# One branch fewer in a fused RWKV-5 attention and balanced-routing kernel: the test on w joins the check after the first search

## The chip, the cores and the metric

The kernel runs on one core of a Trainium2 chip. A core has five instruction streams: TensorE (PE, with weight loads shown apart as PEld), VectorE (DVE), ScalarE (ACT), GpSimd (POOL) and SyncE (SP), which here issues most of the DMAs. The metric is the device time of one execution in microseconds (us); lower is better. Each stream has its own sequencer, so a branch that all five take is five branches, each taken when that engine gets to it.

## The reference

There are two blocks. The first is RWKV-5 attention over r, k, v of shape (4 batches, 8 heads, 768 steps, 48): a state of 48 by 48 per head decays by w and takes in k and v at every step. The second routes the 3072 tokens to 8 experts, 384 tokens each, greedily by logit, and runs a two-layer ReLU network per expert.

```python
for t in range(S):
    cur = np.einsum('bhd,bhe->bhde', u[None] * kt, vt)
    y[:, :, t] = np.einsum('bhd,bhde->bhe', rt, state + cur)
    state = w[None, :, :, None] * state + np.einsum('bhd,bhe->bhde', kt, vt)
...
order = np.argsort(-flat)
for idx in order:
    tok, e = (int(idx) // E, int(idx) % E)
    if assigned[tok] >= 0 or counts[e] >= cap:
        continue
    assigned[tok] = e
    counts[e] += 1
...
h = np.maximum(x[mask] @ w1[e], 0.0)
out[mask] = h @ w2[e]
```

The inputs have w between 0.85 and 0.95.

## The kernel before

**Two attentions.** The attention works in 24 units, one for each of 6 chunks of 128 steps and 4 batches. `attention_mild` (lines 481 to 685) computes a chunk with powers of w taken from the middle of the chunk, which holds for w between 0.7 and 1.2; `attention_any` (lines 28 to 283) holds for every w and is much longer. `Mild.__init__` (line 293) prepares the tables, counts how many w lie within the bounds, writes the answer into a word called `flag` (line 399), does the first steps of units 0 and 1, and loads the flag into a register of every engine (line 421). Line 1261 then branches on it. These inputs take the first arm, so every engine falls into it, and at its end each engine executes an unconditional branch over the code of the other arm. In the trace both kinds stand as `COMPARE_BRANCH` of line 1261.

**Per unit** TensorE turns r and k (`rows_turned`, `keys_turned`), multiplies pairs (`pairs`, line 526), and forms outputs that stay transposed in `turned[n]` (line 571). VectorE scales k by w (`scale`, line 439), masks the products (line 528) and sums the diagonal (`own`, line 453); GpSimd multiplies r, k and u; ScalarE writes diagonals (line 458) and copies. The order on the engines is written out by hand under `manual_schedule`.

**The first search.** The logits of all tokens lie in `LG`. `Assignment.search` looks for the first expert that fills: `likely` (line 950) runs three rounds of `count` (line 881), each a compare on VectorE, three small products on TensorE, sums on VectorE, one more product, and more sums. Then `tokens` (line 1150) turns the result into a list of token numbers, `tok`. A word, also called flag (line 1032), says whether the quick search was right.

**Rows of x in the search's gaps.** The result of the attention has to lie in DRAM by rows (`x_rows`) before tokens can be gathered from it. `rows` (line 608) takes one unit, turns it with four transposes into one of four PSUM banks, copies it on ScalarE (line 619) and stores it from SP (line 621). Its calls are put into gaps of the search: one unit ahead of the last logits, three after them, then two or three at each `between` inside `count`, and what is left after line 1016. After the last product of `tokens` (line 1177), `between(0)` puts four products on TensorE whose results nobody reads (line 681); five more of this kind follow at line 1438, past the join of the two arms.

**After the search** SP loads the number of the expert and issues the first half of its first weights (line 1229, 768 KB). `settle` (line 921) has GpSimd gather the tokens' rows in three indirect DMAs (line 1238), loads the search's flag on every engine (line 926), and branches (line 928): when the flag is 0, a slow exact search (`surely`) and new gathers are made; these inputs skip that. `leave` (line 937) takes the filled expert out. Then the experts follow: `opening` for the first (transposes of gathered rows at line 1317, their copy by ScalarE at line 1318, products at line 1328), with the search for the next expert between its products.

**Skipping an arm.** A skipped arm leaves no gap in the counting of semaphores: the engine that skips it executes a short block that waits for what it had issued before and adds to each semaphore what the arm would have added. Instructions after the join that follow on memory used in the arm wait for those added counts.

## Time and profile before

| | |
|---|---|
| median of 4 runs | 408.96 us (408.77 to 409.15) |
| the profiled execution | 409.54 us, of which the span of its instructions is 407.8 us |
| granted TensorE clock, mean | 0.997 |
| PE busy | 391.2 us, 96% of the span |
| DVE, ACT, POOL busy | 261.7, 147.1, 118.4 us |
| DMA | 54.43 MB, mean 133 GB/s |

All times below are microseconds from the start of the span. A row of the timeline gives the start of a group of equal instructions, how long it lasted, the engine, the source line, the operation and its tiles; in brackets stands how long the engine had been idle and what ended that. An engine name with a q behind it (SPq, PEldq) is the engine's sequencer: branches, semaphore waits and DMA issues. Matmuls are in float32, so one product of the program stands as two rows of weight loads and two of matmuls.

### The profile page before, as it was taken

The page shows a single profiled execution, that of the slowest core. Times are in us where ns is not written, and L with a number is a line of the kernel's source. Part 1 is how long each engine was busy: PE and PEld are TensorE (multiplying, and loading weights), DVE is VectorE, ACT ScalarE, POOL GpSimd, SP SyncE. Part 2 cuts the span into 40 slices and gives each one's busy share as a digit, 9 for nine tenths or more (in the row PEclk, how much of TensorE's full clock was granted, in tenths as well). Part 3 has the DMA queues.
Part 4 walks back from the last instruction along what each step waited for, and adds up shares of the span by engine and source line. Part 5 has one row for each costly group of instructions (what it writes and reads, how often), then busy time and mean ns, then how long its engine had stood idle before and what let it go on. Part 6 is the DMA issues. An engine that isn't in the chain of part 4 may idle for free. (4 is left out here: it accounts for less than half of the span.)

```text
span 407.8 us, 8503 instructions
## 1 busy us (share of the span) xinstructions
PE 391.2 (96%) x3174; PEld 289.3 (71%) x3174; DVE 261.7 (64%) x767; ACT 147.1 (36%) x378; POOL 118.4 (29%) x154
## 2 busy tenths in 40 slices
PE   7999999999987899999999999999999999999993
PEld 4788888888876585865775785685595586587583
DVE  6997889877567278588478568657856836321021
ACT  3897877878656021212112112112121121211200
POOL 6855775657000302220320320310202122201001
PEclk9999999999999999999999999999999999999998
DMA  8979996810039465614711810830651497201001
GB/s 166 202 146 201 188 197 137 162 34 3 3 130 335 144 233 176 214 39 150 239 39 59 295 73 3 267 129 32 200 188 41 159 341 236 58 21 39 0 21 39
DMA packets 93996, 54.43 MB, mean 133 GB/s; under 512 B 76784, under 2 KB 88176, under 8 KB 93936
## 3 DMA queue, kind: packets, MB, share of 16 engines
q1 hardware_dynamic: 89280, 41.70, 37.1%
q0 software_dynamic: 3072, 9.44, 7.0%
q10 hardware_dynamic: 1584, 2.56, 1.8%
q8 instruction: 29, 0.48, 0.5%
q14 instruction: 31, 0.25, 0.2%
HBM read 44.25 MB, written 9.44 MB: 132 GB/s over the span
## 5 line engine op out<-in xcount | busy, mean ns | idle before, releaser
L1328 PE MATMUL h_ps<-xT,w 128*128 128x384 f32 (+1 forms) x372 | 121.8, 475 | 0.0
L1328 PEld LDWEIGHTS h_ps<-xT,w 128*128 128x128 f32 x372 | 64.6, 190 | 35.9 <-issue 4.0
L1335 ACT ACTIVATE hid<-h_ps 128x384 f32<-128x384 f32 x56 | 27.5, 490 | 114.5 <-PE h_ps L1328 101.0
L1238 POOL DMA_INDIRECT xg<-x_rows,tok x24 | 24.9, 1039 | 144.4 <-issue 121.2
L458 ACT ACTIVATE AT<-ident,dd 128x128 f32<-128x128 f32 x188 | 58.1, 392 | 0.0
L1378 POOL DMA_INDIRECT out_dram<-o_sb,tok x24 | 26.6, 1108 | 104.3 <-DVE o_sb L1428 64.6
L1386 PE MATMUL o_ps<-w,hid 128*128 128x384 f32 x128 | 44.4, 493 | 0.9
L528 DVE COPY_PREDICATED AT<-mask,g_ps 128x512 f32<-128x512 uint8 x48 | 32.6, 732 | 7.5 <-PE g_ps L526 6.7
L1386 PEld LDWEIGHTS o_ps<-w,hid 128*128 128x128 f32 x128 | 23.5, 190 | 18.4 <-issue 4.4
L1407 PE MATMUL o_ps<-T,S 128*128 128x192 f32 x192 | 32.6, 327 | 0.0
L1407 PEld LDWEIGHTS o_ps<-T,S 128*128 128x128 f32 x192 | 31.4, 190 | 0.2 <-DVE S L1399 0.2
L526 PE MATMUL g_ps<-rT,kT 48*128 48x128 f32 x384 | 27.9, 285 | 0.1
L450 POOL TENSOR_TENSOR rk<-rk,u_bc 128x384 f32<-128x384 f32 x24 | 27.3, 1139 | 1.9
L449 POOL TENSOR_TENSOR rk<-rt,kt 128x384 f32<-128x384 f32 x24 | 25.5, 1064 | 5.7 <-DMA rt<-in_r_dram 5.7
L526 PEld LDWEIGHTS g_ps<-rT,kT 48*128 48x128 f32 x384 | 23.3, 187 | 4.1 <-issue 2.9
L571 PE MATMUL y_ps<-AT,vt 128*64 128x128 f32 x368 | 24.6, 276 | 0.0
L1407 PE MATMUL o_ps<-w,hid 128*128 128x192 f32 x128 | 24.6, 326 | 0.0
L1318 ACT COPY xT<-xT_ps 128x384 f32<-128x384 f32 x24 | 10.8, 481 | 34.4 <-PE xT_ps L1317 34.4
L1407 PEld LDWEIGHTS o_ps<-w,hid 128*128 128x128 f32 x128 | 20.9, 190 | 2.1
L470 DVE TENSOR_TENSOR rT<-rT_ps,wr 128x512 f32<-128x512 f32 x24 | 16.5, 687 | 7.6 <-PE rT_ps L465 7.4
L571 PEld LDWEIGHTS y_ps<-AT,vt 128*64 128x64 f32 x368 | 19.7, 137 | 0.9 <-issue 0.3
L1412 DVE TENSOR_TENSOR both<-o_ps,one 128x192 f32<-128x192 f32 x8 | 2.9, 357 | 26.8 <-ACT one L1419 26.8
(237 smaller groups left out, 587.3 us busy)
## 6 DMA issues: line engine op xcount, KB each, us to landing
w<-in_moe_w_dram SPq DMA_DIRECT2D x14, 1536.0 KB, 7.4
kt<-in_k_dram SPq DMA_DIRECT2D x24, 192.0 KB, 3.5
rt<-in_r_dram SPq DMA_DIRECT2D x24, 192.0 KB, 3.7
vt<-in_v_dram SPq DMA_DIRECT2D x24, 192.0 KB, 3.6
x_rows<-AT SPq DMA_DIRECT2D x8, 192.0 KB, 2.8
w<-in_moe_w_dram ACTq DMA_DIRECT2D x1, 1536.0 KB
x_rows<-rt SPq DMA_DIRECT2D x6, 192.0 KB, 3.6
x_rows<-ks SPq DMA_DIRECT2D x5, 192.0 KB, 2.7
```

What stands on the lines that cost most here:

```text
L449: nc.gpsimd.tensor_mul(rk, rt[:, :, 0:D], kt)
L450: nc.gpsimd.tensor_mul(rk, rk, self.u_bc.rearrange("p (h d) -> p h d", h=H))
L458: self.tc.nc.scalar.activation(AT[:, h % 2, h // 2, :], self.ident, AF.Copy, scale=dd[:, h:h + 1])
L526: nc.tensor.matmul(g_pss[q][:, a, :], kT[heads[q], a, :], rT[heads[q], a, :], start=True, stop=True)
L528: nc.vector.copy_predicated(out=AT[:, q], mask=mask.unsqueeze(1).to_broadcast([128, HP, T]), data=g_pss[q])
L571: nc.tensor.matmul(y[j][halves[i], g, :], vt[:, 2 * a + j, :], AT[:, j, a, :], start=(c == 0 and g == 0), stop=(g == 1), skip_group_check= ...
L1238: nc.gpsimd.indirect_dma_start(out=xg[:, c, :], out_offset=None, in_=x_dram, in_offset=bass.IndirectOffsetOnAxis(ap=tok[:, c:c + 1], axis=0))
L1328: product = nc.tensor.matmul(h_ps[:, cols], w1[:, f, ts(j, 128)], xT[:, f, cols], start=(f == 0), stop=(f == KD - 1))
L1335: nc.scalar.activation(hid[:, j, :], h_ps, AF.Relu)
L1378: nc.gpsimd.indirect_dma_start(out=out_rows[n * NC + c], out_offset=bass.IndirectOffsetOnAxis(ap=tok[:, c:c + 1], axis=0), in_=o_sb, in_of ...
L1386: nc.tensor.matmul(o_ps, hid[:, j, ts(c, 128)], w2[:, j, :], start=(j == 0), stop=(j == KF - 1))
L1407: nc.tensor.matmul(part, a[:, j, :], b[:, j, :], start=(j == 0), stop=(j == HF - 1))
```

## The change

1. The branch of line 1261 goes. `Mild` keeps its flag; after the first search a product on VectorE multiplies the search's flag by it, and `settle` of the first search, which had its branch anyway, now also covers a w out of bounds: its body calls `attention_any` first (`anew`) and then the exact search and the gathers. So a chip on which w is within bounds runs one long straight stream from the start to that branch. The branch comes before the pools of the experts are opened, and the gathers stand before it in the same block as the search.
2. `attention_any` no longer borrows memory from `Mild`, nor runs the search itself.
3. `rows` works by half units: 2 transposes a step, the copy and the store after the second half. It is called with 2 and 7 halves around the last logits (1 and 3 units before), with 4 and 7 halves in the gaps of `count` (2 and 3 units before), and with all the rest at the end.
4. The unread products become 9 ahead of the branch (4 before) and 1 after it (5 before).
5. `mild.scale(2)` is tied behind `mild.own(1)`, which is the order that the branch had made, and the zeros of `remainder`, a memset, are computed from `taken`, which keeps them from being moved ahead.

With the branch on w gone, what the skipped body would have done is larger: on SP the short block behind the branch waits for and adds to all eight DMA semaphores that SP uses, that of the half of the weights among them (one semaphore before); on GpSimd, VectorE, ScalarE and TensorE it adds their own counts. In the built program the first copy of gathered rows on ScalarE (line 1318 of the kernel before) waits for these added counts of SP's eight semaphores, of VectorE and of GpSimd; before, it waited for none that an engine adds after this branch, other than TensorE's.

```diff
-            self.holds = nc.values_load(flag[0:1, 0:1])
...
-    todo = iter(range(N))
+    todo = iter([(n, half) for n in range(N) for half in range(2)])
...
-            n = next(todo, None)
+            n, half = next(todo, (None, 0))
...
-            for a in range(HP):
+            for a in (2 * half, 2 * half + 1):
                 nc.tensor.transpose(xr_ps[:, a, :], turned[n][:, a, :], ident)
+            if half == 0:
+                continue
...
             mild.step_products(2)
-            mild.scale(2)
+            with tc.issue_after(mild.summed):
+                mild.scale(2)
...
-            rows(1)
+            rows(2)
             logits(C - 1)
             by_token(C - 1)
-            rows(3)
+            rows(7)
...
         def between(most):
-            rows(most or N)
+            rows({2: 4, 3: 7}.get(most, 2 * N))
             if not most:
-                for _ in range(4):
+                for _ in range(9):
                     nc.tensor.matmul(g_pss[0][:, 0:3, :], ident, ident.unsqueeze(1).to_broadcast([128, 3, 128]),
...
         with self.tc.If(found < 1):
+            if anew:
+                anew()
             with ExitStack() as part:
...
-        nc.vector.memset(sel[:, 1, :], 0.0)
+        nc.vector.tensor_single_scalar(out=sel[:, 1, :], in_=self.taken, scalar=0.0, op=ALU.mult)
...
         walk.search(ahead)
+        nc.vector.tensor_mul(ahead["flag"][0:1, :], ahead["flag"][0:1, :], mild.flag)
         ask_half(ahead["fmax"])
...
+    arguments = tc, r, k, v, w, u, moe_w_gate
     with ExitStack() as part:
-        mild = Mild(part, tc, r, k, v, w, u, moe_w_gate, ident)
-        arguments = (tc, r, k, v, w, u, moe_w_gate, x_dram, LG, ident, walk, first)
-        with tc.If(mild.holds > 0) as branch:
-            with ExitStack() as arm:
-                attention_mild(arm, tc, mild, *arguments[1:])
-        with branch.Else():
-            with ExitStack() as arm:
-                attention_any(arm, mild.vts + mild.rts + mild.kss, mild.ATs[0:2], *arguments)
+        mild = Mild(part, *arguments, ident)
+        with ExitStack() as arm:
+            attention_mild(arm, mild, *arguments, x_dram, LG, ident, walk, first)
+
+    def anew():
+        with ExitStack() as arm:
+            attention_any(arm, *arguments, x_dram, LG, ident, walk)
 
     walk.open(ctx)
+    walk.settle(ahead, ask_half, fetch(xg), asked=True, anew=anew)
...
     awake = ps_t.tile([128, KD, 128], F32, name="xT_ps")
-    for _ in range(5):
-        nc.tensor.matmul(awake, ident, ident.unsqueeze(1).to_broadcast([128, KD, 128]), start=True, stop=True)
-    walk.settle(ahead, ask_half, fetch(xg), asked=True)
+    nc.tensor.matmul(awake, ident, ident.unsqueeze(1).to_broadcast([128, KD, 128]), start=True, stop=True)
```

## The prediction

> **What bounds the kernel now.** I read the page first (busy shares, the chain of waits), then the stages by windows, then the timeline of the stage that the change touches, then the branch instructions by line.

> ```profile
> PE 391.2 (96%) x3174; PEld 289.3 (71%) x3174; DVE 261.7 (64%) x767; ACT 147.1 (36%) x378; POOL 118.4 (29%) x154
> ...
> 114.00:131.30 17.30, 14.13 (x149) 12.12 (x147) 13.63 (x63) 11.12 (x25) 0.00 (x0) 1.00 0.70 251
> 131.30:140.40 9.10, 7.45 (x24) 3.81 (x25) 1.92 (x11) 0.48 (x1) 3.06 (x3) 1.00 0.67 206
> 140.40:158.30 17.90, 17.34 (x120) 13.73 (x120) 12.75 (x52) 4.39 (x9) 0.00 (x0) 1.00 0.47 159
> 158.30:400.00 241.70, 239.97 (x1087) 168.48 (x1088) 141.19 (x447) 43.70 (x94) 46.53 (x43) 1.00 0.37 125
> ```

> Each window's row gives its length, then busy time of PE, PEld, DVE, ACT and POOL. From 140.40 on PE works 257.3 of 259.6 us, so whatever moves the first expert's products moves the end as far. The stretch to read is 131.30 to 140.40: of its 7.45 us of PE work, all but the transposes at 139.16 are unread products.

> ```profile
> 131.26 0.18 PE L1177 MATMUL list_ps<-part,alike 128*128 128x12 f16 x1 [0.57 <-DVE part L1175]
> 131.30 2.83 PE L681 MATMUL g_ps<-ident 128*128 128x384 f32 x8
> 131.92 0.41 SPq L1229 DMA_DIRECT2D w<-in_moe_w_dram  x1
> 134.57 1.17 POOL L1238 DMA_INDIRECT xg<-x_rows,tok  x1 [31.86 <-issue]
> 135.43 3.46 PE L1438 MATMUL xT_ps<-ident 128*128 128x384 f32 x10 [1.31 <-issue]
> 139.16 0.31 PEld L1317 LDWEIGHTS xT_ps<-ident,xg 128*128 128x128 f32 x3 [0.88 <-DMA xg<-x_rows,tok]
> 139.87 0.48 ACT L1318 COPY xT<-xT_ps 128x384 f32<-128x384 f32 x1 [9.53 <-PE xT_ps L1317]
> 140.40 1.42 PEld L1328 LDWEIGHTS h_ps<-xT,w 128*128 128x128 f32 x12 [0.66 <-ACT xT L1318]
> ```

> List of tokens, four unread products, 1.31 us of nothing, five more, then transposes, copy, and the expert's first product at 140.40. The branches, by line:

> ```profile
> L1261 ACTq COMPARE_BRANCH  x1: 38/38/38, 129.9 to 129.9; - x1
> L1261 PEldq COMPARE_BRANCH  x1: 3946/3946/3946, 131.3 to 131.3; - x1
> L1261 DVEq COMPARE_BRANCH  x1: 57/57/57, 131.7 to 131.7; - x1
> L1261 SPq COMPARE_BRANCH  x1: 43/43/43, 132.4 to 132.4; - x1
> ...
> L926 ACTq TENSOR_LOAD <-flag x1: 291/291/291, 132.7 to 132.7; - x1
> L926 SPq TENSOR_LOAD <-flag x1: 281/281/281, 138.5 to 138.5; - x1
> ...
> L928 POOLq COMPARE_BRANCH  x1: 58/58/58, 135.6 to 135.6; - x1
> L928 POOLq EVENT_SEMAPHORE  x1: 43/43/43, 135.8 to 135.8; - x1
> L928 PEldq COMPARE_BRANCH  x1: 242/242/242, 135.9 to 135.9; - x1
> ```

> The reader sees what a jump over an arm costs each sequencer: ACT 129.9 to its next instruction at 132.7, 2.8 us; PE 3.9; DVE from 131.7 to its first wait of line 1122 at 134.7, 2.9; SP, behind its own 768 KB of weights, 132.4 to 138.5, 6.1. GpSimd's short jump of line 928 costs 0.1.

> **The change, part by part.** All times against the profiled execution.

> *The branch at 12 us and its register loads: 0.* DVE goes without a gap through that moment (rows from 11.73, 12.33, 13.15, 13.61 to the masking at 14.43), and PE next waits for that masking (idle 0.17 at 15.84, ended by it). Without that cover it would be worth the 0.27 us that PE idles at 12.79; bounds 0 and a gain of 0.27. SP's load and branch (21.07 to 21.7) go too, so loads start 0.8 us sooner; GpSimd waited for loads at most 3.23 us (25.86), but PE keeps a period of 3.5 and then 4.1 us per unit, so 0. The tie of the third scaling keeps DVE's order: 0.

> *Rows by halves: no PE time, the last store 0.5 sooner.* Before each count PE waits 0.52 to 0.58 us for DVE; one half (2 transposes, 0.22 us) more in it costs nothing. After line 1016 three units are left, not five. ACT's last copy ends near 129.5 in place of 130.34, but SP's issues (0.49 apart, 18 after 120.97) bound the stores, and only its waits for ACT near 125 and 126.5 (0.5 and 0.3) go, so the last issue ends near 130.6 in place of 131.10. The gather waits for these stores: from 134.57 to about 134.0. Bounds 0 and 0.8.

> *The product of the flags: +0.1 on DVE*, queued ahead of `row` in the token list. Nearest rows: the small operations around it start 0.09 to 0.12 apart and last 0.15 to 0.18, so 0.09 to 0.18. The list's product moves from 131.30 to 131.40.

> *Nine unread products, then the branch.* Five take 3.46, four 2.83, so each more 0.63 to 0.65; nine take 6.0, to 137.4. PE's register load (0.31) and jump (3.95) run beside them if the queue takes the products in: 131.4 to about 135.9, 1.5 us of cover. The trace shows seven products of the program queued when PE loads the flag at 158.4. Were only five taken, the jump would start after four have run, at 133.9, and end at 138.2: bounds 0 and 0.8. I take 0, as seven is the nearer. From the end of the products to the next matmul 0.27 (138.89 to 139.16): 137.7. One product: 0.65, to 138.3.

> [...]

> *The transposes:* the first gather's 4.2 us to landing, from 134.0, gives 138.2, so it is in time. Transposes at 138.35, and from their start to the copy 0.71 (139.16 to 139.87): 139.1.

> *The added wait on that copy.* ScalarE now waits until SP and GpSimd have added the skipped counts; behind it in ACT's queue stand the second copy, the issue of the weights' second half and the activations, and PE waits for the copy. SP: weights issued at 131.4, load and branch to 132.3, jump 6.1 (same queue, same 768 KB in front) to 138.4. Then ten waits that add; SP's two of line 928 are 0.1 apart, so 0.6 to 1.0, and I take 0.8: 139.2. One more wait on ACT: the copy at 139.3. With a jump like those of the other engines (2.8 to 3.9) SP would be bound by the landing of the weights (6.2 after issue, 137.6), and PE's 139.1 would decide. GpSimd: load and branch stood 1.08 behind the start of the first gather, so 135.1; its jump over the longer body 2.8 to 2.9 (ACT, DVE): 138.0. Bounds for GpSimd 0.1 (its own row) and 6.1 (SP's).

> [...]

> *DVE* reaches `leave` near 135.8 and not 138.85, worth 0: its first count stands behind nine of the expert's products in PE's order, and the row of the first sum shows it waiting 1.63 us for PE already. *The zeros of `remainder`*: 0.15 on DVE in the last expert's list, beside products; 0 to 0.1.

> *Sum.* The first expert's product follows the copy by 0.53: 139.8 in place of 140.40, 0.6 us sooner; a span of 407.2 and an execution of 408.9 by the profile's own 409.54. That execution stands 0.6 above the median 408.96, so on the median's scale 408.4. Its own range: 408.0 (no replay on the path, 0.2 more; the flags' product free, 0.1; early 0.1) to 408.8.

> **Rivals.** A measurement of this kernel tells about 0.2%, 0.8 us, from no change.

> *Faster by more than that (0.25).* SP's jump is not held up, the flags' product hides, the stores land 0.8 sooner and part of the 0.27 at 12.79 is kept: 0.6 + 0.2 + 0.1 + 0.1, about 408.0, at most 407.7. For it: SP's 6.1 is a single row. Against: each is a bound, not a middle.

> *No gain (0.13).* PE's jump too falls behind the weights, since SP now issues them before PE and DVE branch and not after: 131.8 + 6.1 = 138.0 for PE, product, transposes, copy at 139.6 to 139.8; 408.7 to 408.9. This is also where the queue of five leads.

> *Slower (0.12): the copy waits for GpSimd.* If GpSimd's jump takes SP's 6.1, it adds its count at 141.2, the copy starts at 141.3 against 139.87 and the end comes 1.4 later: 410.4. It decides from a jump of 4.1 on, and slows the kernel from 4.7 on. For it: DMA is 0.67 busy in this stage, and the gathers start together with that jump. Against: the weights' data, by what the jump follows them, have left by then.

> **How the numbers follow.** The middle case has 0.50. Faster by over 0.2% (below 408.14): the first rival and a little of the middle, 0.27. Within: 0.62. Slower (above 409.78): most of the last rival, 0.11. The range is 407.7 to 409.7: below it nothing that I can price, above it the slower half of GpSimd's case.

> **What would show it.** Right: no branch rows near 12 us; nine unread products in one run from 131.4, the next within 0.4 us of their end; the weights issued near 131.4; ACT's copy near 139.3, its long wait ended by SP's added counts; the first expert's product near 139.8, and the rest unchanged. Wrong: an idle PE ahead of the product of line 1437, or a copy that follows GpSimd's branch. The prediction fails if the long straight stream costs PE elsewhere: the periods of 3.5 and 4.1 us per unit, or the 2.3 us that PE idles after 140.40, would then change.

## The result, and the profile after

The changed kernel takes 410.07 us (median of 52 executions, 408.79 to 411.39), the kernel before 409.01 beside it; the ratio is 1.0021 (95% interval 1.0014 to 1.0029). So it is slower by about 0.9 us, where 0.6 faster was forecast. The profiled execution took 410.21 us, its span is 408.5.

The page of the changed kernel, the clock that TensorE was granted, in tenths of full speed and 40 slices of the span:

```profile
PEclk9999999999999899999999999999999999999998
```

One slice has an 8. The same windows as before the change say where (length; busy time of PE, PEld, DVE, ACT, POOL; granted clock; DMA share; GB/s):

```profile
114.00:131.30 17.30, 14.13 (x149) 12.18 (x147) 13.58 (x64) 11.11 (x25) 0.00 (x0) 1.00 0.75 271
131.30:140.40 9.10, 8.80 (x25) 4.83 (x26) 2.95 (x13) 0.00 (x0) 3.06 (x3) 0.81 0.54 170
140.40:158.30 17.90, 17.85 (x118) 13.69 (x117) 11.28 (x48) 4.87 (x10) 0.00 (x0) 1.00 0.42 144
158.30:400.00 241.70, 239.95 (x1092) 168.48 (x1091) 142.04 (x449) 43.69 (x94) 46.16 (x43) 1.00 0.37 126
```

In the stretch that the change touches the clock is 0.81 in place of 1.00, and PE is busy for 8.80 us in place of 7.45. The timeline of that stretch, PE and the copy:

```profile
130.35 0.31 PE L1165 MATMUL some_ps<-vals,row 128*128 128x48 f16 x6 [1.44 <-DVE vals L875]
131.23 0.18 PE L1175 MATMUL list_ps<-part,alike 128*128 128x12 f16 x1 [0.57 <-DVE part L1173]
131.27 7.75 PE L677 MATMUL g_ps<-ident 128*128 128x384 f32 x18
139.31 0.88 PE L1437 MATMUL xT_ps<-ident 128*128 128x384 f32 x2 [0.30 <-PEq L924]
140.03 0.49 PE L1317 MATMUL xT_ps<-ident,xg 128*128 128x128 f32 x3
140.68 0.48 ACT L1318 COPY xT<-xT_ps 128x384 f32<-128x384 f32 x1 [11.25 <-PE xT_ps L1317]
141.21 1.60 PE L1328 MATMUL h_ps<-xT,w 128*128 128x128 f32 x12
```

The nine unread products take 7.75 us, not 6.0. Ahead of the products that make the list (the first row above) PE now idles 1.44 us, where it idled 0.56. In the kernel before, transposes of `rows` stood closer in front of them:

```profile
129.22 0.60 PE L617 MATMUL kv_ps<-ident,xT 128*128 128x128 f32 x4
130.38 0.31 PE L1167 MATMUL some_ps<-vals,row 128*128 128x48 f16 x6 [0.56 <-DVE vals L879]
```

The first expert's product stands at 141.21: 9.98 us behind the list's product (131.23), against 9.14 before (131.26 to 140.40). The branch has this form (line 924; min, median and max over the seven experts, and the first and last start):

```profile
L924 PEldq COMPARE_BRANCH  x7: 202/218/5974, 131.9 to 324.2; - x7
L924 DVEq COMPARE_BRANCH  x7: 56/63/72, 132.3 to 326.3; - x7
...
L924 POOLq COMPARE_BRANCH  x7: 45/45/58, 134.8 to 326.3; - x7
L924 DVEq EVENT_SEMAPHORE  x7: 21/21/21, 137.2 to 326.8; - x7
L924 POOLq INC_SWDGE_SEM  x7: 259/536/904, 138.2 to 326.5; - x7
```

PE's jump, the time that its sequencer needs to go on behind the skipped body, takes 5.97 us (3.95 before); it is over at 137.9, here still beside the slow products. VectorE's lasts from 132.3 to 137.2. GpSimd adds its counts only at 138.2.

The whole span falls into four parts: up to the list's product; from there to the first expert's; from there to the end of PE's last product (the start of its last row in the timeline and its length, 399.63 + 1.46 before, 399.84 + 1.46 after); and what follows. In us, with the kernels of the experiments that come below:

| kernel | list to first expert | to PE's last product | after it | ratio to before |
|---|---|---|---|---|
| before | 9.14 | 260.69 | 6.74 | |
| changed | 9.98 | 260.09 | 7.19 | 1.0021 (1.0014 to 1.0029) |
| whole_rows | 9.32 | 260.61 | 7.19 | 1.0037 (1.0022 to 1.0052) |
| fill_gap | 9.26 | 260.21 | 7.19 | 1.0013 (0.9993 to 1.0032) |
| before_halves | 9.68 | 261.85 | 6.74 | 1.0044 (1.0021 to 1.0067) |
| before_nine | 9.05 | 260.44 | 6.74 | 1.0007 (0.9988 to 1.0026) |
| pad_end | 9.02 | 260.44 | 6.74 | 0.9978 (0.9938 to 1.0017) |
| short_body | 8.29 | 259.61 | 6.71 | one execution, 407.9 us |
| short_body_timed | 8.29 | 259.92 | 6.71 | 0.9963 (0.9943 to 0.9983) |
| act_asks | 10.73 | 260.22 | 7.19 | 1.0072 (1.0034 to 1.0110) |
| no_branch | 8.14 | 259.58 | 6.71 | 0.9952 (0.9938 to 0.9966) |
| before_parts | 8.63 | 261.29 | 6.74 | 0.9995 (0.9974 to 1.0016) |
| late_ask | 10.30 | 260.50 | 6.74 | 1.0047 (1.0025 to 1.0069) |
| parts_late_ask | 8.87 | 261.22 | 6.74 | 0.9993 (0.9971 to 1.0015) |

Between the two profiled executions the changed kernel loses 0.84 in the stage, wins 0.60 in the long part behind it, and loses 0.45 after PE's last product. The first part is the same to 0.03 us.

### The profile page after: what moved, and what is told of

Its sections match the earlier page's. It is cut to its first block, busy times and chain, and to the rows that moved or that the text cites. A ratio compares the mean times of both kernels' runs of the same rounds, so it can differ in the third digit from the quotient of the medians.

```text
span 408.5 us, 8495 instructions
## 1 busy us (share of the span) xinstructions
PE 393.5 (96%) x3176; PEld 290.8 (71%) x3176; DVE 262.9 (64%) x768; ACT 147.1 (36%) x378; POOL 117.4 (29%) x154
## 5 line engine op out<-in xcount | busy, mean ns | idle before, releaser
L1328 PE MATMUL h_ps<-xT,w 128*128 128x384 f32 (+1 forms) x372 | 121.8, 475 | 0.0
L1328 PEld LDWEIGHTS h_ps<-xT,w 128*128 128x128 f32 x372 | 64.6, 190 | 35.9 <-issue 4.0
L1318 ACT COPY xT<-xT_ps 128x384 f32<-128x384 f32 x24 | 10.8, 480 | 36.1 <-PE xT_ps L1317 36.1
```

The source lines that it names most:

```text
L1328: product = nc.tensor.matmul(h_ps[:, cols], w1[:, f, ts(j, 128)], xT[:, f, cols], start=(f == 0), stop=(f == KD - 1))
```

## The experiments

### The clock: an idle gap, or nine products in a run?

Two theories for the clock of 0.81. A: the gap of 1.44 us ahead of the list makes it fall. B: nine such products in a run do. Two kernels take the gap away and keep the nine; two others put the halves alone, and the nine alone, into the kernel before.

```diff
 whole_rows (on the changed kernel)
-            rows(7)
+            rows(6)
-            rows({2: 4, 3: 7}.get(most, 2 * N))
+            rows({2: 4, 3: 6}.get(most, 2 * N))
 fill_gap (on the changed kernel)
-            if not most:
+            if most not in (2, 3):
-                for _ in range(9):
+                for _ in range(9 if not most else 2):
```

> The changed kernel with the rows by whole units again, spread as before the change, so that five units and not three stand after the search's last product and TensorE idles some 0.6 us and not 1.44 us ahead of the list's first product; the nine unread products stay. Theory A (the idle gap of 1.44 us makes the clock gate halve TensorE's clock for 3.4 us, in which the nine products stand: 7.75 us in place of 6.0): granted clock 1.00 from 131.3 to 140.4, the nine products end near 137.3, the first expert's product follows TensorE's branch (137.9) and stands at 140.0 and not 141.2; median 408.6 to 409.0, about 1.2 below the changed kernel. Theory B (nine such products in one run are what makes the clock fall): the clock falls here too, median as the changed kernel, 410.1.

> The changed kernel with two more unread products behind the last unit's transposes, in the idle gap of 1.44 us ahead of the list's first product. Theory A (idle gap): clock 1.00 from 131.3 to 140.4, the first expert's product near 140.0, median 408.6 to 409.0. Theory B (so many unread products close together): the clock falls as in the changed kernel or more, 410.1 or above.

The timeline of PE, whole_rows:

```profile
130.53 0.31 PE L1165 MATMUL some_ps<-vals,row 128*128 128x48 f16 x6 [0.57 <-DVE vals L875]
...
131.46 6.05 PE L677 MATMUL g_ps<-ident 128*128 128x384 f32 x18
138.34 0.88 PE L1437 MATMUL xT_ps<-ident 128*128 128x384 f32 x2 [0.84 <-PEq L924]
```

and of fill_gap:

```profile
129.36 1.46 PE L677 MATMUL g_ps<-ident 128*128 128x384 f32 x4
130.96 0.31 PE L1165 MATMUL some_ps<-vals,row 128*128 128x48 f16 x6
...
131.88 6.05 PE L677 MATMUL g_ps<-ident 128*128 128x384 f32 x18
138.58 0.88 PE L1437 MATMUL xT_ps<-ident 128*128 128x384 f32 x2 [0.65 <-PEq L924]
139.89 0.52 PE L1317 MATMUL xT_ps<-ident,xg 128*128 128x128 f32 x3 [0.43 <-remote]
```

With the gap gone the nine products take 6.05 us in both traces: A holds and B falls, as far as the clock goes. The time does not follow: 1.0037 and 1.0013, where the time of the kernel before or less was expected of both. The gain stays out because two things stand behind the clock. PE waits for its own jump (0.84 and 0.65 us, ended by its sequencer at line 924), and in fill_gap the transposes wait another 0.43 for a count that GpSimd adds at 139.58. In whole_rows they wait another 0.28; the row puts that down to the gathered rows, but GpSimd's count, added at 139.17, stands just as close in front of them. Of whole_rows, five of its twelve executions took 411.0 to 411.7 us without a low clock, about 1 us above the profiled one's group (410.0 to 410.4); what they lose was not in a profile, and stays open. Two more, of 412.2 and 412.6 us, do show a low mean clock (0.992 and 0.991), which the traced execution gives no reason for.

```diff
 before_halves (on the kernel before): rows by halves as in the change, nothing else
 before_nine (on the kernel before)
-                for _ in range(4):
+                for _ in range(9):
-    for _ in range(5):
+    for _ in range(1):
```

> The kernel before with its rows by half units alone (2 and 7 halves, 4 and 7 halves in the gaps), all else as before. Theory A (idle gap): TensorE idles 1.4 us ahead of the list's first product here too, and in most executions the clock is halved for 3.4 us; the four unread products take some 4.3 us, which fills the 1.31 us that TensorE idled, so the first expert's product comes 0 to 0.7 later: 409.0 to 409.7. Theory B (nine products in one run): clock 1.00, 409.0.

> The kernel before with nine unread products ahead of the branch and one after it, rows by whole units. Theory A (idle gap): clock 1.00; TensorE's jump (131.3 to 135.3) lies beside the nine products, they end near 137.3 and the transposes wait for the gathered rows as before: 408.8 to 409.2. Theory B (nine products in one run): the clock falls after 131.3, the nine end near 139, the first expert's product near 141: 409.7 to 410.3.

before_halves, PE's busy time and clock in the 3.41 us ahead of 131.85, and then by single microseconds (length; PE busy; granted clock; DMA share; GB/s):

```profile
128.43:131.85 3.42, 1.42 (x15) 1.00 0.99 364
131.00:132.00 1.00, 0.65 (x3) 0.92 0.81 303
132.00:133.00 1.00, 1.00 (x2) 0.50 0.47 79
...
135.00:136.00 1.00, 0.91 (x3) 0.87 0.31 113
```

and its timeline of PE:

```profile
130.47 0.31 PE L1169 MATMUL some_ps<-vals,row 128*128 128x48 f16 x6 [1.43 <-DVE vals L881]
...
131.39 4.52 PE L683 MATMUL g_ps<-ident 128*128 128x384 f32 x8
```

before_nine:

```profile
131.44 6.05 PE L681 MATMUL g_ps<-ident 128*128 128x384 f32 x18
137.64 0.88 PE L1438 MATMUL xT_ps<-ident 128*128 128x384 f32 x2
139.21 0.55 PE L1317 MATMUL xT_ps<-ident,xg 128*128 128x128 f32 x3 [0.69 <-DMA xg<-x_rows,tok]
```

The halves alone bring the gap (1.43) and the half clock into the kernel before; its ratio of 1.0044 is more than the 0 to 0.7 us expected. In its trace the stage is only 0.54 us longer; the larger share, 1.16 us, is lost in the long part behind it, where PE waits 1.60 us for the list of the last expert and 0.82 in the kernel before. The nine products alone bring neither gap nor half clock: they take 6.05 us, PE's jump lies hidden beside them, and the transposes wait for the gathered rows as they did before.

How the clock falls can be read from the same kind of rows. The changed kernel:

```profile
129.11:132.52 3.41, 1.60 (x11) 1.00 0.77 275
132.00:133.00 1.00, 1.00 (x4) 0.76 0.48 131
133.00:134.00 1.00, 1.00 (x2) 0.50 0.97 358
...
135.00:136.00 1.00, 1.00 (x3) 0.53 0.58 119
```

A share of 0.76 in 132 to 133 is half speed from 132.52 on, and 0.53 is half speed up to 135.94. Half speed lasts 3.41 us and follows a window of the same length in which PE was busy for 1.60 us, 47%. In the clock records of each trace all changes stand whole multiples of 3.413 us apart (in the changed kernel's 36, 1 and 79 of them, from 9.64 us on), so the windows can be laid through a whole execution. The kernel before, its two emptiest windows in this stage:

```profile
128.70:132.11 3.41, 2.28 (x21) 1.00 0.93 339
132.11:135.53 3.42, 2.11 (x8) 1.00 0.74 236
```

Laid so through all the traces of this study, from the first record of full speed (at 7 to 10 us) to PE's last product, every window in which PE was busy for 47% or less is followed by half speed (before_halves above: 1.42 us, 42%), and every one of 53% or more is not (before_halves from 346.89 on: 1.81 us, 53%). At the start it takes more to leave half speed: in the kernel before, the window from 2.41 to 5.82 us is 88% busy, and half speed still lasts to 9.23 (four matmuls of line 465 take 1.06 us from 6.81 on, and 0.60 from 11.08 on). Where the windows fall differs from one execution to the next, so a gap is hit in some and not in others: pad_end below has the same gap of 1.44 us, but the two windows around it in its trace are 63% and 68% busy, and its clock stays full. In the trace of the changed kernel 57% of all positions have a window below half; in the kernel before and in fill_gap none. The mean clock of an execution shows it roughly: PE's idle end alone (half speed from 405.18 us on in the kernel before, where the trace has 0.997) leaves 0.994 to 0.998, and half speed for 3.41 us takes another 0.004. Of the 54 executions of the changed kernel whose clock is on record 17 show 0.992 or less; their median is 410.69 us, that of the others 409.78. That is 31%, not 57%; the mean doesn't show single windows, and why they differ stays open. Of fill_gap none in twelve is that low.

### The end: a pause of GpSimd

All kernels made from the changed one with a program of 721 GpSimd instructions have 7.19 us after PE's last product, all others 6.71 to 6.74. In the changed kernel GpSimd stands still for 0.42 us between two instructions of the program's end (407.33 to 407.74; 0.09 in the kernel before), and the drain after it takes 0.24 and not 0.11.

```diff
 pad_end (on the changed kernel), in the body that is skipped; 22 instructions as built
+            spot = arm.enter_context(tc.tile_pool(name="spot", bufs=1)).tile([128, 1], F32, name="spot")
+            for _ in range(21):
+                nc.gpsimd.memset(spot, 0.0)
```

> The changed kernel with 22 GpSimd instructions more inside the body that is skipped, none executed, so that GpSimd's last instructions stand where they stood before the change (743 instructions in its program; 742 before, 721 in the changed kernel). Theory E (0.45 us of the slowdown is a pause of GpSimd at the very end, between two instructions after the last store, because of where its program ends): the time from TensorE's last product to the end of the span falls from 7.19 back to 6.74 us, and the median lies 0.4 to 0.5 below the changed kernel's, near 1.001 of the kernel before. Rival (the pause belongs to the larger number of semaphore counts or to something else in the changed program): it stays, 7.19 us.

The drains of GpSimd (number; min, median, max in ns; first and last start), of which the median one stands at this place, in the kernel before and in the changed one:

```profile
L1489 POOLq DRAIN  x3: 45/113/5442, 401.5 to 407.6; - x3
L1487 POOLq DRAIN  x3: 40/241/5448, 401.7 to 408.2; - x3
```

and of pad_end:

```profile
L1490 POOLq DRAIN  x3: 40/113/5447, 401.6 to 407.6; - x3
```

The pause is gone and the part is 6.74 us again, by instructions that never run. So 0.45 us of the slowdown goes when instructions that never run are put ahead of GpSimd's last ones; that it is the place where these stand is the likeliest reading, not a shown one. The ratio itself (0.9978, 0.9938 to 1.0017) is too wide to tell; the medians were 409.77 beside 409.57. Why a place in the program would cost 0.42 us was not tried: no fetch is recorded in that moment.

### The jump: a long body, or weights ahead of its fetch?

PE's jump takes 5.6 to 6.0 us in the changed kernel and 3.95 in the kernel before. Three theories. W: its instruction fetch stands behind the weights that SyncE has asked. B: the body that it skips is long. C: the jump is now conditional, and such a jump takes longer than the unconditional one of before.

```diff
 short_body (on fill_gap)
-    walk.settle(ahead, ask_half, fetch(xg), asked=True, anew=anew)
+    walk.settle(ahead, ask_half, fetch(xg), asked=True)
 act_asks (on fill_gap): the number alone ahead of the branch, and behind it
+    weights(number, w1, slice(0, F // 2), nc.scalar)
 no_branch (on fill_gap), in settle
+        if asked:
+            return self.leave(out["fmax"], out["acc"])
```

> The kernel with the filled gap, its skipped body without the general attention (which is left out; for these inputs it isn't needed), so that TensorE's skipped body is some 1600 instructions shorter. Theory W (TensorE's jump is long because its instruction fetch stands behind the data of the weights, asked 0.8 us ahead of its branch): the jump stays at 5.6 to 6.0 us and the single unread product starts 6.7 us after the list's product. Rival B (the jump is long because the skipped body is long): the jump falls to 3 to 4 us, the single product starts 6.2 to 6.3 after the list's, and the first expert's product comes 0.5 to 0.8 earlier. Rival C (a conditional jump takes longer than the unconditional one of before, whatever it skips): as theory W.

> The kernel with the filled gap, and the first half of the first expert's weights asked by ScalarE behind the branch and not by SyncE ahead of it. Theory W: TensorE's jump takes 3.9 to 4.0 us as in the kernel before, the single product starts 6.2 to 6.3 us after the list's product and not 6.7; the first expert's product then waits for weights that are asked near 135.3 and land some 5.3 later, so the time stays about that of the filled gap (0.1 to 0.3 % above the kernel before). Rivals B and C: the jump stays at 5.6 to 6.0.

> The kernel with the filled gap, without the first search's branch: no flag is loaded, and exact search, general attention and their gathers are left out. What the jumps cost altogether: the single unread product starts 6.2 us after the list's (6.7 with the jump), the transposes follow the gathers, and the first expert's product stands 8.3 us after the list's product and not 9.26; of this 0.9 some half is taken back at the last expert, whose list waits for weights (TensorE idles there 0.8 in the kernel before and 0.3 in the changed one): 0.3 to 0.9 below the filled gap's time. If the jump isn't what holds the changed kernel, nothing moves.

> The kernel with the filled gap and the short body again, timed: the one look gave 407.9 us with TensorE's jump at 0.37 us. Theory (no engine has to fetch for a jump over the short body): as without the branch, 0.9945 to 0.997 of the kernel before, and a spread under 1 us. If the one look was a lucky execution: 0.998 or more.

PE's and GpSimd's rows of line 924, short_body:

```profile
L924 PEldq COMPARE_BRANCH  x7: 207/223/373, 132.1 to 322.6; - x7
...
L924 POOLq COMPARE_BRANCH  x7: 45/45/45, 134.9 to 324.6; - x7
L924 POOLq EVENT_SEMAPHORE  x7: 43/43/43, 135.1 to 324.8; - x7
```

act_asks, PE's row of line 924, and from its timeline what the first expert's product waits for:

```profile
L924 PEldq COMPARE_BRANCH  x7: 202/217/3834, 132.1 to 325.1; - x7
```

```profile
142.16 1.02 PE L1332 MATMUL h_ps<-xT,w 128*128 128x128 f32 x7 [1.72 <-DMA w<-in_moe_w_dram]
```

no_branch:

```profile
131.54 6.05 PE L677 MATMUL g_ps<-ident 128*128 128x384 f32 x18
...
139.65 1.60 PE L1330 MATMUL h_ps<-xT,w 128*128 128x128 f32 x12
```

B and W are both right, one after the other. Over the short body PE's jump takes 0.37 us, SP's, VectorE's and GpSimd's 0.2 to 0.6, and the kernel is as fast as one without the branch: 0.9963 and 0.9952. That is the price of the long body: 1.0 us of the stage (9.26 to 8.29 and 8.14), and 0.3 to 0.6 in the part behind it; another 0.48 goes at the end of these two programs (6.71 against 7.19), which hold fewer GpSimd instructions. Over the long body, with the weights asked later, PE's jump is 3.83 and SP's own, with no weights in front of it, 0.50 (5.0 in the changed kernel): W. But the weights then come too late, and the product waits 1.72 us for them (1.0072).

```diff
 late_ask (on fill_gap with the instructions of pad_end)
-        walk.search(ahead)
+        listed = walk.search(ahead)
-        ask_half(ahead["fmax"])
+        with tc.issue_after(listed):
+            ask_half(ahead["fmax"])
```

> The changed kernel with the filled gap, the 22 instructions for its end, and the first weights asked later: the number of the expert is computed behind the list of tokens, so that SyncE asks near 132.8 and not 131.0. Theory W: TensorE's fetch is ahead of the weights, its jump takes 3.8 to 4.0 us and the single unread product starts 6.2 us after the list's; but SyncE's and GpSimd's jumps still take 5 and 3.1, and the transposes wait for GpSimd's added counts some 7.9 us after the list's product (7.9 in the kernel before): no faster than the kernel before, 0 to 0.1 % above it, and some 0.2 % below the filled gap. If only TensorE's jump mattered: 8.3 us from the list's product to the first expert's, and 0.1 to 0.2 % below the kernel before.

late_ask, its branch and the start of GpSimd's added counts, and then its timeline with the transposes:

```profile
L924 PEldq COMPARE_BRANCH  x7: 202/216/3554, 132.1 to 324.8; - x7
...
L924 POOLq COMPARE_BRANCH  x7: 45/45/58, 135.9 to 326.9; - x7
...
L924 POOLq INC_SWDGE_SEM  x7: 254/532/904, 140.2 to 327.1; - x7
```

```profile
137.77 0.88 PE L1441 MATMUL xT_ps<-ident 128*128 128x384 f32 x2 [0.30 <-PEq L924]
140.47 0.52 PE L1321 MATMUL xT_ps<-ident,xg 128*128 128x128 f32 x3 [1.82 <-remote]
```

PE's jump is 3.55 us and the single product starts 0.30 behind the nine, as W has it. Now GpSimd's jump stands behind the weights: from 135.9 to its first wait at 140.0, 4.1 us, and the transposes wait 1.82 us for the count that it adds at 140.2. The stage takes 10.30 us, where that of the kernel before, 9.14, was expected; the ratio is 1.0047.

### Can the rest of the change win anything?

The kernel before keeps its branch on w; it gets the halves, nine and one products and the filled gap, once with the weights as asked by then, once with them behind the list.

> The kernel before, with its branch on w and the jump over the other arm, plus rows by half units, nine unread products ahead of the branch and one after it, and two more unread products in the idle gap. Theory (what cost the changed kernel is the long body behind the first search's branch, and the idle gap; the two other parts do what they were priced at): TensorE's jump (3.9 us) lies beside the nine products, the clock stays at 1.00, the gathers start some 2.4 us after the list's product and not 3.3, the first expert's product stands 8.3 to 8.6 us after the list's and not 9.1: 0.3 to 0.7 us below the kernel before, ratio 0.998 to 0.9993. If the half units or the split of the unread products are themselves what costs: at or above the kernel before.

> The kernel before with its branch on w, rows by half units, nine and one unread products and the filled gap, and the first weights asked behind the list of tokens (near 132.8 us and not 130.9). Theory W: the fetches for the jump over the other arm are ahead of the weights again: TensorE's jump takes 3.9 us and not 5.9, VectorE's 3 and not 5.6; the single unread product follows the nine (6.2 us after the list's product), VectorE takes the filled expert out before 139, and the first expert's product stands 8.2 to 8.4 us after the list's. GpSimd skips only a short body, so nothing waits for it as it did with the late weights in the changed kernel. 0.4 to 1.0 us below the kernel before, ratio 0.9975 to 0.999. If the jumps stay long, or the weights come too late for the first product: at or above it.

The unconditional jump (line 1261 of the kernel before) in before_parts, first and second start and min, median, max:

```profile
L1263 PEldq COMPARE_BRANCH  x2: 86/2996/5906, 12.6 to 131.4; - x2
```

and in parts_late_ask:

```profile
L1264 PEldq COMPARE_BRANCH  x2: 86/2036/3986, 12.6 to 131.3; - x2
```

This settles W against C: the same unconditional jump takes 5.91 us with the weights asked 0.4 ahead of it and 3.99 with them behind. From the traces, when the weights were asked, when PE branched, when its fetch of 16 KB began (a DMA packet of the kind that the trace calls instruction), and how long the jump took:

| kernel | weights asked | PE branches | fetch begins | jump |
|---|---|---|---|---|
| before | 131.92 | 131.31 | 132.63 | 3.95 |
| before_nine | 131.86 | 131.47 | 132.94 | 3.85 |
| before_halves | 131.26 | 131.38 | 132.77 | 3.97 |
| late_ask | 132.74 | 132.05 | 132.98 | 3.55 |
| whole_rows | 131.98 | 132.37 | 135.35 | 5.61 |
| fill_gap | 131.70 | 132.51 | 135.55 | 5.75 |
| pad_end | 131.36 | 132.34 | 135.33 | 5.81 |
| changed | 130.94 | 131.90 | 134.73 | 5.97 |
| before_parts | 130.94 | 131.36 | 134.25 | 5.91 |

Where the weights are asked 0.4 us or more ahead of PE's branch, its fetch begins 2.8 to 3.0 us after the branch; where they are asked 0.1 ahead or behind it, 0.9 to 1.5. The trace doesn't name the engine of a fetch: those of 16 KB are taken to be PE's, since one begins inside each of these jumps and none inside the 0.37 us of short_body.

Both kernels bring the first expert's product 0.5 and 0.3 us nearer to the list's (8.63 and 8.87), and neither is faster by more than its interval. Their long part is 0.6 and 0.5 us longer, so the gain is taken back behind the stage. In parts_late_ask PE waits 1.30 us for the list of the last expert (0.82 in the kernel before), which VectorE gets to only after the last expert's weights have landed. Why those come later relative to the first expert's product there (VectorE starts on them 205.93 us after it, 205.40 in the kernel before, 204.80 in the changed one) stays open. No version that keeps both attentions and the exact search beats the kernel before clearly.

## Why the prediction was wrong, point by point

**The step that failed first: "Rows by halves: no PE time."** It looked at VectorE's waits, at ScalarE's copies and at SP's issues, and noted that "after line 1016 three units are left, not five", but not what PE would do in their place: 0.9 us more of nothing, 1.44 in place of 0.56. With that the clock is halved for 3.41 us in a part of the executions (17 of 54 by the mean clock), and there the nine products, priced at 6.0 us, take 7.75. The price per product was right (6.05 where the clock is full). In the profile of before the rows that would have told are the 0.56 ahead of line 1167 and the transposes in front of it. Gaps of 1.44 and 0.57 us close together were enough for 3.41 us at a clock of 0.50, so what counts in these runs is a window of 3.41 us less than about half busy (1.60 us in the changed kernel's).

**The step that cost most: the jumps over the long body, PE's first.** "Jump (3.95) run beside them ... 131.4 to about 135.9" became 5.97 us, to 137.9. That is the rival called no gain, with its mechanism and nearly its price (138.0), held at 0.13 chance. The row for it, SP's 6.1 us behind its own weights, was shown and used for SP alone, though halves bring the weights forward (130.94, forecast 131.4) while PE's branch moves back by its register load. It was the jump and GpSimd's counts, not the products, that held the stage where the clock was full (whole_rows, fill_gap, pad_end): 9.02 to 9.32 us, about the 9.14 of before, and not the 8.4 forecast (131.40 to 139.8). That the forecast's 8.4 is there to be had without the jumps over the long body is shown by short_body (8.29) and no_branch (8.14).

**GpSimd's jump.** Forecast 2.8 to 2.9, measured 3.1 (134.83 to 137.96) in the changed kernel; the row of 0.1 did not hold. It was the row of a short body: over that of short_body GpSimd's jump takes 0.2 (134.9 to 135.1), and PE's 0.37, where it takes 5.75 over the long body (fill_gap). The slower rival, a wait for GpSimd "from a jump of 4.1 on", did not come in the changed kernel's profile; fill_gap has it (0.43) with a jump of 3.2, since GpSimd's branch stands there at 136.22 and not at 135.1, and late_ask more of it (1.82), at 4.1 us. In both the transposes wait for GpSimd's count, and not first ScalarE's copy as forecast.

**SP's added counts.** Jump 6.1 and 0.8 for the counts were forecast; 5.0 and some 0.6 (136.75 to 137.34) were measured, and nothing was held up by them: ScalarE's copy came at 140.68 and was waiting for PE.

**The end.** No step had the last 0.45 us. "Whatever moves the first expert's products moves the end as far" holds in direction only: 0.81 later at the first product was 0.21 later at PE's last one (401.09 to 401.30), because the last expert's list waits for weights as well as for PE, which idles 0.28 us ahead of it in the changed kernel and 0.82 in the kernel before.

**What was right.** The branch at 12 us is worth nothing (the list's product at 131.23, before 131.26). The flags' product hides on VectorE, so its 0.1 was one too many. The gathers start sooner in the changed kernel's profile: 133.56, forecast 134.0, before 134.57 (134.94 in fill_gap). PE's queue took the nine products in: its branch starts at 131.90, when one of them has run. None of these runs shows where that queue ends.

Put together, these don't account for the whole. The end costs 0.45 us in the trace, the stage some 0.1 with a full clock (9.26 in fill_gap against 9.14), and 17 of 54 executions lie 0.9 higher, 0.3 on the mean: 0.85, against a measured 0.0021 of 409 us, 0.86. But this sum leaves out the long part behind the stage, which is 0.60 us shorter in the changed kernel's trace and 0.48 in fill_gap's, so that its coming out is luck. The executions without a low clock alone lie 0.77 us above the 409.01 of the kernel before; what takes back the gain of the long part in them is open. Part of it may be that the profiled execution of the kernel before, at 409.54 us, is itself 0.5 above that median.

## What to carry to other kernels

A skipped body isn't free by being skipped: over the long body here PE's jump took 3.55 us or more and held a fetch, over the short one 0.37 and none, and with 768 KB of weights asked 0.4 us or more ahead of the branch PE's fetch began 2.8 to 3.0 us after it, otherwise 0.9 to 1.5; measure the jump of each engine, and ask the load behind the jump only where its data can still come in time (in act_asks the product waited 1.72 us for them). Work moved into earlier gaps leaves a gap where it stood; on TensorE look at how busy windows of 3.4 us are around the place (47% was too little here, 53% was not), not at the single wait. And compare the last microseconds of two programs as well: 0.45 us of this slowdown of about 0.9 stand behind the last product.
